# A gated-attention, spectral-mixing and conv-gate kernel: the weight range check moved behind the decode, the low weight parts moved from GpSimd to VectorE

## The chip, the cores and the metric

One core of one Trainium2 chip runs the whole kernel. The metric is the device time of one execution in microseconds (us). Three runs of the kernel before gave 638.92, 641.32 and 641.36 us; the median is 641.32 us. Engines are named as in the profile: PE (TensorE), DVE (VectorE), ACT (ScalarE), POOL (GpSimd), SP (the engine whose queue issues the loads and stores).

## The reference

Three stages follow one another. All inputs are drawn with a fixed seed; the weights are 64-bit floats, the rest 32-bit.

```python
# 1. gated linear attention, per batch (4) and head (8), 768 steps, head size 48
state = alpha[:, :, t, :, None] * state + np.einsum('bhd,bhe->bhde', k[:, :, t], v[:, :, t])
y[:, :, t] = np.einsum('bhd,bhde->bhe', q[:, :, t], state)
# 2. spectral mixing over the 768 tokens, width 384
theta = x @ w_theta
yr = np.einsum('ts,bsd->btd', w_tok_r, x * np.cos(theta))
yi = np.einsum('ts,bsd->btd', w_tok_i, x * np.sin(theta))
u = x + yr + yi
x = u + np.maximum(u @ w_ch, 0.0)
# 3. MLP (384 -> 1024 -> 384) with a 3-tap convolution over tokens as its gate
h = np.maximum(x @ w_in, 0.0)
out = (h * sigmoid(conv(h, conv_w))) @ w_out
```

## The kernel before

Tokens are worked in 24 chunks of 128 (6 for each of 4 batches). The program is written stage by stage, and a scheduler (`schedule_with_timeline_sim=True`, L632) then sets the order of the instructions on each engine. Every engine works its list in order, and each load is issued from SP's list in order too, so that a load that waits for its buffer holds back the loads behind it.

**Attention.** For chunk `ci`, `a_load` brings `a_t`, `qk_t` and `v_t`. `a_prep` works on DVE: a scan backwards (L216), the starts (L219, L220), a scan forwards (L221), a small product (L222), and the product of queries and keys with both scans (L224). ACT then squares the scans in place for a range check (L225); there is one buffer `fbt`, so the next chunk's first scan waits for this. `a_score` and `a_y` are matmuls, with copies on ACT and a triangular mask on POOL (L239); the state is updated on DVE and POOL (L274, L279).

**Mixing.** `a_theta` multiplies a chunk by `w_theta` (tile `th`), takes cosine and sine on ACT and DVE (tile `zf`), and splits the product into a high and a low part (`zh`, `zl`). `m_mix` multiplies these by `w_tok` (tile `yps`). Every fp32 product is made of three matmuls of such parts (`mm3`), so every weight is split too.

**Weights.** A piece of weights is up to 768 64-bit numbers per partition. `load_split` (L110) loads it into one of two buffers (tile `stage`, STB = 2); `decode` (L94) turns it into fp32 in the same buffer, and `split` (L69) writes high and low part. Step by step: POOL squares the upper words as fp32 (L99); ACT takes the sign of the square less a tiny bound and sums it into a column of `wacc` (L103, and an accumulator read of its own); DVE builds the fp32 word in three instructions (L106, L107, L108); ACT copies the high part (L70); POOL subtracts it to give the low part (L71). The DVE steps write where the sign was written, so they wait for it, and the sign waits for the square. The buffer is free for the next load when POOL has subtracted.

There are 24 pieces: 2 of `w_theta` and 12 of `w_tok` while attention runs (batches 0 and 1), 2 of `w_ch`, 4 of `w_in` and, with the MLP under way, 4 of `w_out`. The 3 taps of the convolution (`conv_w`, L404) are decoded without a split. `count_bad` (L502) compares each column of `wacc` with the number of weights in the piece; if one differs, a slow second program runs after the fast one. POOL writes the 25 wanted numbers (L506).

**Channel matmul and MLP.** `m_ch` (tile `cps`) and `m_in`/`m_out` (tiles `hps`, `ops`) follow, with splits on ACT and DVE and the convolution on ACT and DVE (L474 to L488). The low parts of all activations are subtracted on DVE already (the last argument of `split`).

Of the kernel before, what the change touches and what calls it, by code (L numbers as in the profile page):

```python
# [8 lines left out]
F32 = mybir.dt.float32  # L9
# [5 lines left out]
AF = mybir.ActivationFunctionType  # L15
ALU = mybir.AluOpType
PSUM = bass.MemoryType.PSUM

P = 128
# [6 lines left out]
NF = DFF // P  # L26
# [12 lines left out]
TINY = 2.0**-15  # L39
# [3 lines left out]
def tile_gated_linear_attention__then__spectral_moe__then__conv_gate(  # L43
# [14 lines left out]
    nc = tc.nc  # L58
# [10 lines left out]
    def split(hi, lo, src, lo_eng):  # L69
        nc.scalar.copy(hi, src)  # L70
        lo_eng.tensor_tensor(lo, src, hi.bitcast(F32), ALU.subtract)  # L71
# [3 lines left out]
    wacc = top_p.tile([P, 32], F32, name="wacc")  # L75
# [3 lines left out]
    pieces = []  # L79
# [5 lines left out]
    def body(top, slow):  # L85
# [8 lines left out]
        def decode(full, st, n):  # L94
            words = st[:, : 2 * n].bitcast(U32).rearrange("p (n two) -> p n two", two=2)
            lo, hi = words[:, :, 0], words[:, :, 1]
            hif = hi.bitcast(F32)
            fb = full.bitcast(U32)
            nc.gpsimd.tensor_tensor(full, hif, hif, ALU.mult)  # L99
            if not slow:  # L100
                i = len(pieces)
                pieces.append(n)
                nc.scalar.activation(full, full, AF.Sign, bias=ntiny, accum_out=wacc[:, i : i + 1])  # L103
            else:
                nc.vector.scalar_tensor_tensor(hif, full, TINY * TINY, hif, ALU.is_ge, ALU.mult)
            nc.vector.tensor_scalar(fb, hi, 3, 0x3FFFFFFF, ALU.logical_shift_left, ALU.bitwise_and)  # L106
            nc.vector.scalar_tensor_tensor(fb, hi, 0xC0000000, fb, ALU.bitwise_and, ALU.bitwise_or)  # L107
            nc.vector.scalar_tensor_tensor(fb, lo, 29, fb, ALU.logical_shift_right, ALU.bitwise_or)  # L108

        def load_split(pool, tag, src, shape, out_hi, out_lo, scale=None):  # L110
            n = math.prod(shape)
# [11 lines left out]
            split(out_hi, out_lo, full, nc.gpsimd)  # L123
# [5 lines left out]
        with ExitStack() as ph1:  # L129
# [50 lines left out]
            nc.gpsimd.memset(ntiny, -TINY * TINY)  # L180
# [223 lines left out]
            decode(cw.rearrange("p f k -> p (f k)"), cst, 3 * NF)  # L404
            for c in range(NC):
                m_mix(B - 1, 0, c)
# [95 lines left out]
        def count_bad():  # L502
            np_ = len(pieces)
            want = st_p.tile([P, 32], F32, tag="want", name="want", bufs=1)
            for i, n in enumerate(pieces):
                nc.gpsimd.memset(want[:, i : i + 1], float(n))  # L506
            good = st_p.tile([P, 32 + NCH], F32, tag="good", name="good", bufs=1)
            nc.vector.tensor_tensor(good[:, :np_], wacc[:, :np_], want[:, :np_], ALU.is_equal)
# [128 lines left out]
```

## Time and profile before

| | |
|---|---|
| runs | 638.92, 641.32, 641.36 us; median 641.32 us |
| the profiled execution, first to last instruction (span) | 636.5 us; no other time of this execution is given |
| median less span | 4.8 us |
| PE busy | 598.3 us, 94% |
| DVE busy | 472.9 us, 74% |
| ACT busy | 357.2 us, 56% |
| POOL busy | 159.3 us, 25% |

How to read it: a busy engine is one with an instruction under way, so a stretched instruction counts as busy for as long as it stretches. The busy share of PE is modelled and says little of its speed; the number of matmuls in a stretch and the granted clock beside it say more. Shares over the whole span mix stages that have different limits, so each stage is read by itself. The trace has a stretch for each: 0 to 16 us the fill, 16 to 160 attention with weight loads, 160 to 347 attention and mixing without weight loads, 347 to 448 the loads of the other weights with channel matmul and the first MLP units, 448 to the end the MLP.

### The profile page before, as it was taken

To read this page: it belongs to the slowest core of one execution; us is meant where nothing else is said; L and a number is where in the kernel's file an instruction comes from. 1 tells how busy PE (TensorE), PEld (TensorE's weight loads), DVE (VectorE), ACT (ScalarE), POOL (GpSimd) and SP (SyncE) were. 2 spreads that over 40 slices of the span, in tenths; PEclk is the share of its full clock that TensorE was granted. 3 is DMA by queue.
4 is the path that set the end of the run, shared out by engine and by line. 5 is a ranking of instruction groups with operands and counts; after the bars stand their busy time and mean duration, and the time that the engine had idled before them with its cause. 6 is when DMAs were issued, how large, how long until landed. Compare 5 with 4: busy or idle time off the path is not lost.

```text
span 636.5 us, 9621 instructions
## 1 busy us (share of the span) xinstructions
PE 598.3 (94%) x3703; PEld 576.1 (91%) x3703; DVE 472.9 (74%) x699; ACT 357.2 (56%) x713; POOL 159.3 (25%) x166
## 2 busy tenths in 40 slices
PE   6988797889989999999999999799999999999995
PEld 3978796888979999999999999797999999999995
DVE  6889999997885567843147689999987776777760
ACT  3465665454485346743256343754787767766761
POOL 3367556558301131022100343242100000000000
PEclk8577967987999999999999999899999999999998
DMA  8264344543401333021000321230000001000001
GB/s 296 53 204 161 116 158 113 142 158 104 158 1 36 119 125 97 1 75 59 1 0 27 123 77 51 100 94 5 26 25 26 26 13 38 26 13 25 26 26 42
DMA packets 20805, 47.22 MB, mean 74 GB/s; under 512 B 2064, under 2 KB 8208, under 8 KB 20752
## 3 DMA queue, kind: packets, MB, share of 16 engines
q1 hardware_dynamic: 20752, 46.53, 22.6%
q8 instruction: 31, 0.51, 0.4%
q14 instruction: 22, 0.18, 0.1%
HBM read 41.80 MB, written 4.72 MB: 73 GB/s over the span
## 4 chain that ended last, share of the span: by engine, by line
PE 55%; DVE 18%; ACT 4%; issue 3%; DMA 3%; POOL 1%; SPq 0%; ACTq 0%; DVEq 0%; POOLq 0%
PE ops L62 15%; PE hps L62 13%; PE yps L62 12%; PE y L62 5%; PE th L62 3%; DVE stage L107 2%; PE sc L62 2%; DVE qk_t L224 2%; DVE stage L106 2%; DVE stage L108 1%; DVE x L71 1%; PE cps L62 1%; PE kv L62 1%; DVE us L71 1%; DVE fbt L216 1%
## 5 line engine op out<-in xcount | busy, mean ns | idle before, releaser
L62 PE MATMUL yps<-wtok,zh 128*128 128x384 f32 x576 | 155.4, 350 | 2.2 <-DVE u L347 2.2
L62 PE MATMUL hps<-x,win 128*128 128x386 f32 x576 | 111.7, 342 | 4.6 <-ACT hh L474 4.0
L62 PEld LDWEIGHTS yps<-wtok,zh 128*128 128x128 f32 x576 | 108.4, 197 | 2.8 <-ACT zf L316 2.5
L62 PE MATMUL ops<-wout,g 128*128 128x384 f32 x576 | 109.1, 338 | 0.1
L62 PEld LDWEIGHTS hps<-x,win 128*128 128x128 f32 x576 | 103.1, 191 | 6.0 <-ACT hh L474 5.0
L62 PEld LDWEIGHTS ops<-wout,g 128*128 128x128 f32 x576 | 101.8, 187 | 0.6 <-POOL wout L71 0.4
L62 PE MATMUL yps<-wtok,zl 128*128 128x384 f32 x288 | 98.5, 346 | 0.6 <-DVE zl L71 0.6
L239 POOL TENSOR_SCALAR_AFFINE_SELECT pt<-pt 128x512 f32<-128x512 f32 x48 | 39.5, 845 | 141.3 <-ACT pt L238 141.3
L62 PE MATMUL y<-v_t,pt 128*128 128x48 f32 x384 | 60.3, 289 | 1.8 <-issue 1.5
L62 PEld LDWEIGHTS y<-v_t,pt 128*128 128x128 f32 x384 | 57.2, 217 | 2.7 <-issue 1.7
L225 ACT ACTIVATE fbt<-fbt 128x1024 f32<-128x1024 f32 x24 | 25.5, 1062 | 57.3 <-DVE qk_t L224 49.4
L62 PEld LDWEIGHTS yps<-wtok,zl 128*128 128x128 f32 x288 | 56.1, 195 | 0.9 <-DVE zl L71 0.9
L479 DVE SCALAR_TENSOR_TENSOR cv<-hh,cw,cv 128x383 f32<-128x383 f32 (+1 forms) x64 | 43.3, 679 | 17.3 <-ACT cv L476 16.8
L99 POOL TENSOR_TENSOR stage<-stage 128x768 f32<-128x768 f32 (+1 forms) x24 | 41.1, 1717 | 36.4 <-DMA stage<-in_w_out_dram 14.4
L62 PE MATMUL th<-wth,zh 128*128 128x384 f32 x216 | 46.1, 358 | 1.8 <-DVE zh L71 1.8
L71 DVE TENSOR_TENSOR g<-cv,g 128x384 fp32r<-128x384 f32 x64 | 36.4, 569 | 13.3 <-ACT g L70 12.3
L70 ACT CAST g<-cv 128x384 fp32r<-128x384 f32 x64 | 32.7, 510 | 20.7 <-DVE cv L486 19.3
L216 DVE TENSOR_TENSOR_SCAN fbt<-a_t,onehot 128x512 f32<-128x512 f32 x24 | 30.9, 1287 | 16.7 <-ACT fbt L225 13.3
L486 DVE SCALAR_TENSOR_TENSOR cv<-cv,hh 128x384 f32<-128x384 f32 x64 | 36.6, 573 | 8.9 <-ACT cv L485 7.2
L62 PE MATMUL cps<-us,wch 128*128 128x384 f32 x216 | 42.5, 348 | 0.7 <-DVE us L71 0.7
L224 DVE TENSOR_TENSOR qk_t<-qk_t,fbt 128x1024 f32<-128x1024 f32 x24 | 36.4, 1518 | 8.7 <-DMA qk_t<-in_qka_dram 8.4
L476 ACT ACTIVATE cv<-hh,cw 128x384 f32<-128x384 f32 x64 | 39.2, 616 | 6.5 <-DVE g L71 3.8
(91 smaller groups left out, 997.5 us busy)
## 6 DMA issues: line engine op xcount, KB each, us to landing
qk_t<-in_qka_dram SPq DMA_DIRECT2D x24, 512.0 KB, 4.2
stage<-in_w_tok_dram SPq DMA_DIRECT2D x12, 768.0 KB, 4.6
a_t<-in_qka_dram SPq DMA_DIRECT2D x24, 260.0 KB, 2.8
v_t<-in_v_dram SPq DMA_DIRECT2D x24, 192.0 KB, 3.3
out_dram<-ob SPq DMA_DIRECT2D x24, 192.0 KB, 1.9
stage<-in_w_in_dram SPq DMA_DIRECT2D x4, 768.0 KB, 4.9
stage<-in_w_out_dram SPq DMA_DIRECT2D x4, 768.0 KB, 4.4
stage<-in_w_theta_dram SPq DMA_DIRECT2D x1, 768.0 KB, 9.3
```

Source lines behind the costliest of these rows:

```text
L62: nc.tensor.matmul(o, lhsT, rhs, start=start, stop=stop, skip_group_check=True)
L70: nc.scalar.copy(hi, src)
L71: lo_eng.tensor_tensor(lo, src, hi.bitcast(F32), ALU.subtract)
L99: nc.gpsimd.tensor_tensor(full, hif, hif, ALU.mult)
L106: nc.vector.tensor_scalar(fb, hi, 3, 0x3FFFFFFF, ALU.logical_shift_left, ALU.bitwise_and)
L216: nc.vector.tensor_tensor_scan(bf[:, CW - 1 :: -1], ash[:, CW - 1 :: -1], of[:, CW - 1 :: -1], 0.0, ALU.mult, ALU.add)
L224: nc.vector.tensor_tensor(qt, qt, fl, ALU.mult)
L225: nc.scalar.activation(fl, fl, AF.Square, accum_out=bacc[:, ci : ci + 1])
L239: nc.gpsimd.affine_select(pt, pt, [[0, NP], [1, P]], ALU.is_ge, 0.0, base=0, channel_multiplier=-1)
L476: nc.scalar.activation(cv, hh[:, o : o + HALF], AF.Copy, scale=cw[:, f, 1:2])
L479: nc.vector.scalar_tensor_tensor(cv[:, a:HALF], hh[:, o + a - 1 : o + HALF - 1], cw[:, f, 0:1], cv[:, a:HALF], ALU.mult, ALU.add)
L486: nc.vector.scalar_tensor_tensor(cv, cv, 1.0, hh[:, o : o + HALF], ALU.add, ALU.mult)
```

## The change

The square on POOL (L99) is dropped from the fast program, and the sign is no longer ahead of the decode. A new function `judge` stands behind the split: it takes the sign of the upper word less the bound, and the sign of its negative less the bound, in two ACT instructions that read every second word of the buffer, write the other words (the lower ones, used by then), and sum into two columns. Where all weights lie outside the bound, the two sums cancel; `count_bad` adds the columns and compares with zero. The low part of every weight is subtracted on DVE in place of POOL. The buffer is free for the next load when the second sign is done.

```diff
--- before.py
+++ after.py
@@ -72,7 +72,7 @@
 
     top_p = ctx.enter_context(tc.tile_pool(name="top", bufs=1))
     dram_p = ctx.enter_context(tc.tile_pool(name="xd", bufs=1, space=bass.MemoryType.DRAM))
-    wacc = top_p.tile([P, 32], F32, name="wacc")
+    wacc = top_p.tile([P, 2, 32], F32, name="wacc")
     bacc = top_p.tile([P, NCH], F32, name="bacc")
     flag = top_p.tile([1, 1], I32, name="flag")
     x_dram = dram_p.tile([B, S, DM], F32, name="x_dram")
@@ -96,16 +96,23 @@
             lo, hi = words[:, :, 0], words[:, :, 1]
             hif = hi.bitcast(F32)
             fb = full.bitcast(U32)
-            nc.gpsimd.tensor_tensor(full, hif, hif, ALU.mult)
-            if not slow:
-                i = len(pieces)
-                pieces.append(n)
-                nc.scalar.activation(full, full, AF.Sign, bias=ntiny, accum_out=wacc[:, i : i + 1])
-            else:
+            if slow:
+                nc.gpsimd.tensor_tensor(full, hif, hif, ALU.mult)
                 nc.vector.scalar_tensor_tensor(hif, full, TINY * TINY, hif, ALU.is_ge, ALU.mult)
             nc.vector.tensor_scalar(fb, hi, 3, 0x3FFFFFFF, ALU.logical_shift_left, ALU.bitwise_and)
             nc.vector.scalar_tensor_tensor(fb, hi, 0xC0000000, fb, ALU.bitwise_and, ALU.bitwise_or)
             nc.vector.scalar_tensor_tensor(fb, lo, 29, fb, ALU.logical_shift_right, ALU.bitwise_or)
+
+        def judge(st, n):
+            if slow:
+                return
+            words = st[:, : 2 * n].rearrange("p (n two) -> p n two", two=2)
+            i = len(pieces)
+            pieces.append(n)
+            for j, sgn in enumerate((1.0, -1.0)):
+                nc.scalar.activation(
+                    words[:, :, 0], words[:, :, 1], AF.Sign, bias=ntiny, scale=sgn, accum_out=wacc[:, j, i : i + 1]
+                )
 
         def load_split(pool, tag, src, shape, out_hi, out_lo, scale=None):
             n = math.prod(shape)
@@ -120,7 +127,8 @@
                 nc.scalar.activation(full, full, AF.Copy, scale=scale)
             if len(shape) == 2:
                 full = full.rearrange("p (a n) -> p a n", a=shape[0])
-            split(out_hi, out_lo, full, nc.gpsimd)
+            split(out_hi, out_lo, full, nc.vector)
+            judge(st, n)
 
         ub, xs, zs = {}, {}, {}
 
@@ -177,7 +185,7 @@
             nc.vector.memset(onehot, 0.0)
             nc.vector.memset(onehot[:, :, P - 1 : P], 1.0)
             nc.vector.memset(starts, 0.0)
-            nc.gpsimd.memset(ntiny, -TINY * TINY)
+            nc.gpsimd.memset(ntiny, -TINY)
             for t in Sst:
                 nc.gpsimd.memset(t, 0.0)
             nc.gpsimd.memset(magic, MAGIC)
@@ -402,6 +410,7 @@
             cst = st_p.tile([P, 9 * 256], F32, tag="w", name="cst", bufs=STB)
             nc.sync.dma_start(out=cst[:, : 6 * NF].bitcast(U32), in_=conv_w.rearrange("p f k -> p (f k)").bitcast(U32))
             decode(cw.rearrange("p f k -> p (f k)"), cst, 3 * NF)
+            judge(cst, 3 * NF)
             for c in range(NC):
                 m_mix(B - 1, 0, c)
             tok0_ctx.close()
@@ -501,11 +510,10 @@
 
         def count_bad():
             np_ = len(pieces)
-            want = st_p.tile([P, 32], F32, tag="want", name="want", bufs=1)
-            for i, n in enumerate(pieces):
-                nc.gpsimd.memset(want[:, i : i + 1], float(n))
+            both = st_p.tile([P, 32], F32, tag="both", name="both", bufs=1)
+            nc.vector.tensor_tensor(both[:, :np_], wacc[:, 0, :np_], wacc[:, 1, :np_], ALU.add)
             good = st_p.tile([P, 32 + NCH], F32, tag="good", name="good", bufs=1)
-            nc.vector.tensor_tensor(good[:, :np_], wacc[:, :np_], want[:, :np_], ALU.is_equal)
+            nc.vector.tensor_scalar(good[:, :np_], both[:, :np_], 0.0, None, ALU.is_equal)
             nc.vector.tensor_scalar(good[:, np_ : np_ + NCH], bacc, BIG, None, ALU.is_le)
             bad = st_p.tile([P, 2], F32, tag="bad", name="bad", bufs=1)
             nc.vector.tensor_reduce(bad[:, 0:1], good[:, : np_ + NCH], mybir.AxisListType.X, ALU.min)
```

The scheduler orders the new list anew. Three places show what moves. `stage` is a weight buffer, `fbt` the scans, `qk_t` queries and keys, `wtok` the split token weights; a number behind a name tells buffers and chunks apart.

DVE, near the last pieces of `w_tok`. Before, the last piece is decoded just ahead of the product of the 14th chunk (`qk_t_1264`):

```order
L106 TENSOR_SCALAR stage_1320<-stage_1320 128x768
L107 SCALAR_TENSOR_TENSOR stage_1320<-stage_1320 128x768
L274 TENSOR_TENSOR tst_1223<-S0_112,kv_1218 112x384
L108 SCALAR_TENSOR_TENSOR stage_1320<-stage_1320 128x768
L71 TENSOR_TENSOR zh_1432<-u_857,zh_1432 128x384
L224 TENSOR_TENSOR qk_t_1264<-qk_t_1264,fbt_1608 128x1024
```

Now it is decoded and split ahead of the product of the 11th chunk (`qk_t_986`):

```order
L102 TENSOR_SCALAR stage_1320<-stage_1320 128x768
L71 TENSOR_TENSOR wtok11_88<-stage_1232,wtok10_87 128x2x384
L103 SCALAR_TENSOR_TENSOR stage_1320<-stage_1320 128x768
L224 SCALAR_TENSOR_TENSOR fbt_1084<-a_t_984,onehot_110 128x512
L104 SCALAR_TENSOR_TENSOR stage_1320<-stage_1320 128x768
L282 TENSOR_TENSOR tst_948<-S1_113,kv_943 112x384
L71 TENSOR_TENSOR zl_777<-zf_770,zh_757 128x768
L227 TENSOR_SCALAR starts_111<-fbt_1084 128x4
L228 RECIPROCAL starts_111<-starts_111 128x4
L229 SCALAR_TENSOR_TENSOR fbt_1084<-a_t_984,starts_111 128x512
L230 TENSOR_TENSOR ftot_1085<-a_t_984,fbt_1084 128x4
L71 TENSOR_TENSOR wtok11_88<-stage_1320,wtok10_87 128x2x384
```

All weight work of the attention stage stands some three chunks earlier, and the chunks behind it follow one another on DVE with no weight work between them.

ACT, at the fourth and fifth piece of `w_tok`, as it is now:

```order
L70 CAST wtok00_85<-stage_543 128x2x384
L113 ACTIVATE stage_543,wacc_60<-stage_543,ntiny_75 128x768
L233 ACTIVATE fbt_581,bacc_61<-fbt_581 128x1024
L324 ACTIVATE zf_466<-th_456,magic_114 128x384
L113 ACTIVATE stage_543,wacc_60<-stage_543,ntiny_75 128x768
L70 CAST wtok00_85<-stage_635 128x2x384
L113 ACTIVATE stage_635,wacc_60<-stage_635,ntiny_75 128x768
```

The two signs of a piece stand behind its high part, one ahead of the square of the scans (L233) and one behind it.

SP, the loads around the same pieces. Before, a load of `stage` waits for POOL:

```order
L116 DMA stage_444<-in_w_tok_dram 128x2x768 [waits DMAHW7_49,Pool_49]
L116 DMA stage_543<-in_w_tok_dram 128x2x768 [waits DMAHW0_49,Pool_49]
L199 DMA qk_t_577<-in_qka_dram 128x1024 [waits DMAHW1_49,PE_49]
L201 DMA v_t_480<-in_v_dram 128x384 [waits DMAHW2_49,PE_49]
L197 DMA a_t_801<-in_qka_dram 128x520 [waits DMAHW3_49,DVE_49]
```

Now it waits for ACT:

```order
L123 DMA stage_543<-in_w_tok_dram 128x2x768 [waits DMAHW7_49,Activation_49]
L207 DMA qk_t_478<-in_qka_dram 128x1024 [waits PE_49]
L209 DMA v_t_381<-in_v_dram 128x384 [waits PE_49]
L123 DMA stage_635<-in_w_tok_dram 128x2x768 [waits DMAHW0_49,DMAHW3_49,DVE_49,Activation_49]
L205 DMA a_t_667<-in_qka_dram 128x520 [waits DMAHW1_49,DVE_49]
```

The loads of the same pieces stand one to two chunks earlier among the loads of `qk_t`, and what holds them is the second sign.

## Rows read from the trace of the kernel before

**Rows 1.** Busy us by stretch: PE, PEld, DVE, ACT, POOL (instructions), PEclk, DMA share, GB/s.
```profile
16.00:160.00 144.00, 126.55 (x780) 118.53 (x779) 132.96 (x153) 79.37 (x155) 87.00 (x61) 0.78 0.43 134
160.00:192.00 32.00, 29.81 (x200) 28.30 (x199) 25.60 (x37) 20.97 (x40) 6.30 (x5) 1.00 0.23 74
192.00:347.00 155.00, 155.00 (x1132) 150.85 (x1131) 81.96 (x124) 77.10 (x149) 22.99 (x38) 1.00 0.18 53
...
384.00:448.00 64.00, 58.59 (x305) 55.16 (x304) 61.52 (x94) 34.59 (x72) 22.23 (x12) 0.95 0.16 53
448.00:608.00 160.00, 160.00 (x911) 159.72 (x910) 124.68 (x229) 114.50 (x241) 0.48 (x1) 1.00 0.07 25
```
**Rows 2.** The chain that ended last: start us, us, what.
```profile
123.18 2.86 DVE qk_t L224
```
**Rows 3.** DVE groups, 16 to 176 us: count, busy us, mean ns, idle before.
```profile
L224 DVE TENSOR_TENSOR qk_t<-qk_t,fbt 128x1024 f32<-128x1024 f32 x14 | 24.1, 1725 | 1.8 <-DMA qk_t<-in_qka_dram 1.6
...
L107 DVE SCALAR_TENSOR_TENSOR stage<-stage 128x768 uint32<-128x768 uint32 (+1 forms) x14 | 15.7, 1129 | 0.1
L106 DVE TENSOR_SCALAR stage<-stage 128x768 uint32<-128x768 uint32 (+1 forms) x14 | 14.0, 1002 | 2.5 <-ACT stage L103 2.4
...
L321 DVE TENSOR_TENSOR zf<-x,zf 128x768 f32<-128x768 f32 x6 | 10.8, 1796 | 0.5 <-ACT zf L320 0.5
...
L219 DVE TENSOR_SCALAR starts<-fbt 128x4 f32<-128x4 f32 x14 | 7.0, 501 | 0.3
L222 DVE TENSOR_TENSOR ftot<-a_t,fbt 128x4 f32<-128x4 f32 x13 | 6.5, 502 | 1.7 <-POOL S L279 1.7
```
**Rows 4.** DVE groups, 192 to 347 us, where no weights are worked on.
```profile
L321 DVE TENSOR_TENSOR zf<-x,zf 128x768 f32<-128x768 f32 x14 | 13.4, 958 | 7.0 <-ACT zf L320 6.9
L71 DVE TENSOR_TENSOR zl<-zf,zh 128x768 fp32r<-128x768 f32 x13 | 12.3, 954 | 2.0 <-ACT zh L70 2.0
L224 DVE TENSOR_TENSOR qk_t<-qk_t,fbt 128x1024 f32<-128x1024 f32 x8 | 9.8, 1229 | 6.8 <-DMA qk_t<-in_qka_dram 6.8
...
L222 DVE TENSOR_TENSOR ftot<-a_t,fbt 128x4 f32<-128x4 f32 x9 | 1.5, 165 | 6.1 <-POOL S L279 6.0
...
L219 DVE TENSOR_SCALAR starts<-fbt 128x4 f32<-128x4 f32 x8 | 1.4, 171 | 0.2
```
**Rows 5.** All weight pieces' decode steps: ns min/median/max, first and last start us.
```profile
L106 DVE TENSOR_SCALAR stage<-stage x24: 351/552/2106, 18.4 to 438.9; 128x768 uint32<-128x768 uint32 x22, 128x384 uint32<-128x384 uint32 x2
L107 DVE SCALAR_TENSOR_TENSOR stage<-stage x24: 550/957/2504, 22.5 to 441.0; 128x768 uint32<-128x768 uint32 x22, 128x384 uint32<-128x384 uint32 x2
```
**Rows 6.** POOL in order of time at 379 us, then DVE at the same time.
```profile
378.75 1.85 POOL L71 TENSOR_TENSOR win<-stage,win 128x768 fp32r<-128x768 f32 x1 [4.04 <-ACT win L70]
380.56 1.78 POOL L99 TENSOR_TENSOR stage<-stage 128x768 f32<-128x768 f32 x1
...
379.12 4.11 DVE L71 TENSOR_TENSOR x<-u,x 128x386 fp32r<-128x386 f32 x3 [0.39 <-ACT x L70]
...
383.62 0.55 DVE L71 TENSOR_TENSOR x<-u,x 128x386 fp32r<-128x386 f32 x1
```
**Rows 7.** POOL groups, 16 to 176 us.
```profile
L71 POOL TENSOR_TENSOR wtok<-stage,wtok 128x768 fp32r<-128x768 f32 x12 | 27.2, 2267 | 22.6 <-ACT wtok L70 22.2
L99 POOL TENSOR_TENSOR stage<-stage 128x768 f32<-128x768 f32 x12 | 23.9, 1995 | 8.8 <-DMA stage<-in_w_tok_dram 8.6
L239 POOL TENSOR_SCALAR_AFFINE_SELECT pt<-pt 128x512 f32<-128x512 f32 x24 | 22.8, 969 | 14.8 <-ACT pt L238 14.8
L279 POOL TENSOR_TENSOR S<-tst,ftot 48x192 f32<-48x192 f32 x16 | 16.0, 999 | 6.7 <-DVE tst L274 3.3 <-ACT kt L247 2.6
```
**Rows 8.** ACT groups, 16 to 176 us.
```profile
L103 ACT ACTIVATE stage<-stage,ntiny 128x768 f32<-128x768 f32 (+1 forms) x13 | 11.8, 910 | 5.4 <-POOL stage L99 5.4
L70 ACT CAST wtok<-stage 128x768 fp32r<-128x768 f32 x12 | 10.0, 834 | 13.7 <-DVE stage L108 13.7
...
L103 ACT ACTIVATION_READ_ACCUMULATOR stage<-stage,ntiny 128x1 f32 x14 | 2.7, 190 | 0.0
```

## The prediction, made before the changed kernel ran

> **What bounds the kernel now.** I read the stretches first, then the chain, then the engines' groups, and last two engines side by side in time. The stretches [rows 1] show two limits. From 192 to 347 us and from 448 to 608 us PE is busy throughout at the full granted clock (1.00, the upper of its two levels, 2.4 GHz) while DVE is busy 82 of 155 and 125 of 160 us: nothing that DVE, ACT or POOL do there sets the time. From 16 to 160 us it is the other way: DVE is busy 133 of 144 us, PE's granted clock is 0.78 and it finishes 780 matmuls in 144 us (5.4 per us) against 1132 in 155 (7.3 per us) of about the same mixture behind. This is the front stage, in which attention and 14 of the 24 weight pieces share DVE. From 160 us on PE is nearly full again (29.8 of 32 us, clock 1.00). The second stretch with a loss is 384 to 448 us: 305 matmuls in 64 us, which at the MLP's rate (911 in 160 us, 5.69 per us) would take 53.6 us, so some 10 us are lost there, and DVE is busy 61.5 of the 64 us. The chain of waits agrees: between 101 and 182 us it is mostly DVE, and one of its steps is a product of 2.86 us [rows 2] that elsewhere takes 1.23 [rows 4]. So the time is set by DVE in two stages and by PE in the rest; a microsecond taken from DVE in the first comes back until PE is the limit, and in the second up to 10 us.
>
> **Why DVE is so full.** The same instructions take longer in the front stage than where no weights are worked on. Counts times the undisturbed mean, taken from the busy time [rows 3, 4, 5]: L224 24.1 - 14 x 1.229 = 6.9 us; L106 14.0 - 14 x 0.552 (its median) = 6.3; L321 10.8 - 6 x 0.958 = 5.1; L219 7.0 - 14 x 0.171 = 4.6; L222 6.5 - 13 x 0.165 = 4.4; L107 15.7 - 14 x 0.957 = 2.3. Together 29.6 us, in which DVE counts as busy and does nothing more. What they run beside is seen at 379 us: three subtractions of 0.55 us each (1.65) take 4.11 us, while POOL goes through a subtraction and a square of 1.85 and 1.78 us; they end as POOL ends [rows 6]. Instructions of four elements (L219, L222) are drawn out to half a microsecond on average, so it is waiting and not slower work.
>
> **The change, part by part, front stage (14 pieces).**
> - POOL loses its square and its subtraction. Which part of the 29.6 us goes with them is not shown by a row, so it is bounded: none (the remaining mask and state updates stretch DVE as much), or all. Between: what an instruction waits behind another grows with that one's length, so I weigh POOL's busy time with its mean length [rows 7]: L71 27.2 x 2.27 = 62 and L99 23.9 x 2.00 = 48, against L239 22.8 x 0.97 = 22 and L279 16.0 x 1.00 = 16. The two that go have 110 of 148, 74%. I take 22 us.
> - DVE gains the 14 subtractions. The same form is there, 128x768 from two fp32 operands in 0.954 us [rows 4]: 12 of `w_tok` and one of `w_theta` at that, one half as long, 12.9 us. All of it counts, since DVE is the limit there.
> - DVE no longer waits for the sign ahead of L106: 2.4 us in this stage [rows 3].
> - ACT: the sign moves behind the decode and becomes two, each with its accumulator read: 14 x (0.910 + 0.190) = 15 us more [rows 8]. ACT's 79 of 144 us [rows 1] become some 95. This is covered while ACT is the looser engine; not covered, it is rival 2. New in it is that the sign reads every second word. No ACT row shows that; a gain is excluded, as it handles the same 768 elements; the bounds are 0.91 us as now and 1.82 us, as if it walked over the skipped words too. I take 0.91, because DVE's L107 reads every second word and its median is 0.957 us, no more than the 0.954 us of the subtraction on packed words [rows 4, 5].
> - The wait that is added: a load of `stage` now waits for the second sign, and behind it in SP's list wait loads of `a_t` and `qk_t`, which DVE needs. From the end of the decode that is a high part and two signs, 0.83 + 2 x 1.10 = 3.0 us on ACT [rows 8], against high part and POOL's subtraction, 0.83 + 2.27 = 3.1 us, before [rows 7, 8]; and the square and sign ahead of the decode (2.0 + 1.1 us) are gone. So a buffer turns round about 3 us sooner, if ACT takes the signs at once. I cost it at nothing; its cover is that 3 us.
> - The order: the weight pieces now end ahead of the 11th chunk's product instead of the 14th's. It shifts work within the stage and adds none. The preparations behind run alone, and each then waits for ACT's square of the one `fbt`; I allow 1 us for that.
>
> Sum for the front stage: -22 + 12.9 - 2.4 + 1 = about -10.5 us. PE can follow: at its rate behind (7.3 per us) the 780 matmuls would take 107 of the 144 us, and from 160 us on it is bound by itself, so what DVE gains ahead is gained.
>
> **Weight stage (347 to 448 us, 10 pieces).** POOL does nothing there but this. The three splits at 379 us alone lose 4.11 - 1.65 = 2.5 us to it [rows 6]. Against that stand 10 subtractions on DVE, 9.1 us, and 11 us more of ACT, which is busy 35 of 64 us [rows 1]. Each piece has two steps fewer on POOL between its landing and its use. The gain is at most PE's 10 us of loss, and it is below nothing if the 9.1 us weigh more on DVE than what goes; I take half of the loss, 5 us, since DVE is relieved and loaded at once and the earlier weights let PE start the MLP sooner.
>
> **Without effect.** 25 fills of `want` on POOL and the comparison at the end of `count_bad`: nothing waits for them until the flag is read. The MLP from 448 us and the stretch 192 to 347 us: PE's, untouched.
>
> Total: 10.5 + 5 = about 16 us off. The profiled execution's span of 636.5 us becomes about 620.5; the median of the runs stands 4.8 us above that span, which I leave: **625 us**.
>
> **The rivals.**
> 1. *More comes back.* All 29.6 us go, and groups I left out add some; PE loses nothing in the weight stage. -29.6 + 12.9 - 2.4 = -19, and -10: 612 us. For it: POOL's remaining instructions are themselves drawn out. Against: they stay, and so does what they cost DVE.
> 2. *ACT takes DVE's place.* All the weight work of the front stage now falls into its first two thirds, and ACT with it. Each high part, sign and square stands in one list; a sign of up to 1.82 us adds up to 28 x 0.91 = 25 us to ACT there. Then DVE waits for high parts and squares, and the load queue for the second sign: the front stage gains 2 us instead of 10.5, the weight stage keeps its 5: 634 us. For it: the order puts a sign ahead of the square. Against: ACT has some 50 us to spare.
> 3. *Slower: DVE is full and is given more.* The delays stay and move to the POOL instructions that remain, so DVE has 12.9 us more in the front stage and PE as much longer to wait, less the 2.4; the weight stage loses some 4: 641 + 10.5 + 4 = 656 us. It decides where less than 10.5 of the 29.6 us go. Against it: the mask and the state update are half as long as what goes [rows 7], and in 192 to 347 us they are there and L224 and L219 keep 1.229 and 0.171 us [rows 4]. The Trainium skill (Perfetto Trace Analysis, Optimizing Scalar/DVE Operations) speaks for this rival: where VectorE is saturated, move work off it to ScalarE or even GpSimd; the change does the opposite, and by that rule the stage would lengthen. The same passage adds that moving work between those two might not help because they share a read port; the 4.11 us of three subtractions [rows 6] fit that half.
> 4. *It does not do what it says.* If the two sums did not cancel for weights in range, the slow program would run behind the fast one and the time would be a multiple. For a weight beyond the bound the signs are +1 and -1, whatever the sign of the weight.
>
> **How the numbers follow.** The forecast 0.50; rival 1 0.18; rival 2 0.15; rival 3 0.08; rival 4 0.01; and 0.08 that gains and waits about cancel. About 0.5% (3.2 us) is what a measurement here can tell from no change. Faster: 0.50 + 0.18 + 0.15 = 0.83; same 0.08; slower 0.09. The range of 610 to 640 holds the forecast with its bounds, rivals 1 and 2 and half of the undecided case; outside stay rival 3, rival 4 and some of each end, together under 0.2.
>
> **What would show it.** Right: L224, L219, L222 and L321 near 1.23, 0.17, 0.17 and 0.96 us in the front stage; the weights' subtraction on DVE near 0.95 us; POOL without L99 and L71; PE full from about 150 us instead of 160; more matmuls per us where 384 to 448 us was. Wrong: those means stay up (rival 3); the sign well over 0.94 us, or DVE idle behind ACT's squares and high parts, or behind `qk_t` loads (rival 2); matmuls slower in the MLP, where I expect no change.

## The result, and the profile after

The changed kernel takes 615.48 us (median of 4 runs, 613.1 to 618.19) against 640.12 us (median of 4, 638.14 to 641.36): a ratio of 0.962, with a 95% interval of 0.9589 to 0.9651. The forecast was 625 us in a range of 610 to 640. The profiled execution has a span of 612.1 us, 3.4 us under the median; before it was 636.5. That is 24.4 us less.

Where they went is read from three points of the trace. The first load of `w_ch`, with which the weight stage begins, moves from 347.4 to 333.3 us: the front stage gives 14.1 us. From there to the start of the last matmul of `ops` it was 281.9 us (629.3 less 347.4) and is 272.2 (605.5 less 333.3): the weight stage gives 9.7. The remaining 0.6 us lie in the tail. Before, then after:

```profile
L116 SPq DMA_DIRECT2D stage<-in_w_ch_dram x2: 379/424/468, 347.4 to 347.8; - x2
L62 PE MATMUL ops<-wout,g x576: 331/338/443, 418.8 to 629.3; 128*128 128x384 f32 x192
```
```profile
L123 SPq DMA_DIRECT2D stage<-in_w_ch_dram x2: 379/420/462, 333.3 to 333.7; - x2
L62 PE MATMUL ops<-wout,g x576: 331/338/343, 401.4 to 605.5; 128*128 128x384 f32 x192
```

The stretches, with the columns of [rows 1]:

```profile
16.00:160.00 144.00, 124.32 (x865) 116.64 (x865) 124.53 (x179) 100.85 (x197) 42.72 (x40) 0.87 0.49 151
160.00:192.00 32.00, 32.00 (x224) 30.93 (x224) 21.37 (x32) 22.30 (x42) 3.10 (x6) 1.00 0.09 24
...
384.00:448.00 64.00, 63.34 (x358) 62.17 (x357) 58.23 (x112) 47.69 (x101) 0.00 (x0) 1.00 0.11 35
```

In the front stage PE finishes 865 matmuls instead of 780, its granted clock is 0.87 instead of 0.78, and DVE issues 179 instructions instead of 153 in less busy time (124.5 against 133.0 us). From 384 to 448 us there are 358 matmuls instead of 305, which is 5.59 per us, near the 5.69 of the MLP [rows 1]; counted from the stage's own start, 14 us earlier (370 to 434 us), there are 358 too. POOL is idle there.

When PE becomes the limit is seen in finer windows of the changed kernel:

```profile
112.00:124.00 12.00, 10.27 (x74) 8.87 (x74) 11.10 (x16) 9.47 (x18) 4.46 (x4) 0.86 0.47 145
124.00:136.00 12.00, 11.64 (x97) 11.00 (x97) 9.07 (x16) 6.15 (x13) 3.69 (x5) 1.00 0.34 102
136.00:148.00 12.00, 12.00 (x93) 11.64 (x92) 6.29 (x12) 4.80 (x10) 4.29 (x8) 1.00 0.47 158
```

PE is full from about 125 us, where DVE falls from 11.1 to 9.1 and then 6.3 of 12 us. The DVE groups of 16 to 160 us, which hold the same 14 chunks as [rows 3]:

```profile
L232 DVE TENSOR_TENSOR qk_t<-qk_t,fbt 128x1024 f32<-128x1024 f32 x14 | 17.5, 1252 | 2.7 <-DMA qk_t<-in_qka_dram 2.6
L224 DVE TENSOR_TENSOR_SCAN fbt<-a_t,onehot 128x512 f32<-128x512 f32 x14 | 17.5, 1252 | 5.7 <-ACT fbt L233 5.7
L103 DVE SCALAR_TENSOR_TENSOR stage<-stage 128x768 uint32<-128x768 uint32 (+1 forms) x13 | 13.3, 1027 | 0.0
...
L71 DVE TENSOR_TENSOR wtok<-stage,wtok 128x768 fp32r<-128x768 f32 x12 | 11.7, 972 | 0.0
L102 DVE TENSOR_SCALAR stage<-stage 128x768 uint32<-128x768 uint32 x12 | 7.2, 601 | 3.2 <-DMA stage<-in_w_tok_dram 3.2
...
L329 DVE TENSOR_TENSOR zf<-x,zf 128x768 f32<-128x768 f32 x6 | 5.9, 975 | 0.0
...
L227 DVE TENSOR_SCALAR starts<-fbt 128x4 f32<-128x4 f32 x14 | 3.6, 254 | 0.1
...
L230 DVE TENSOR_TENSOR ftot<-a_t,fbt 128x4 f32<-128x4 f32 x13 | 2.4, 187 | 2.9 <-POOL S L287 2.9
...
L71 DVE TENSOR_TENSOR wth<-stage,wth 128x768 fp32r<-128x768 f32 (+1 forms) x2 | 1.5, 752 | 0.0
```

The product of queries and keys takes 1.252 us on average instead of 1.725, the product with `zf` 0.975 instead of 1.796, the four-element instructions 0.254 and 0.187 instead of 0.501 and 0.502. The subtraction that came to DVE takes 0.972 us. POOL and ACT in the same stretch, answering to [rows 7] and [rows 8]:

```profile
L247 POOL TENSOR_SCALAR_AFFINE_SELECT pt<-pt 128x512 f32<-128x512 f32 x24 | 27.4, 1159 | 94.2 <-ACT pt L246 94.1
L287 POOL TENSOR_TENSOR S<-tst,ftot 48x192 f32<-48x192 f32 x16 | 15.4, 962 | 7.2 <-DVE tst L282 6.5
```
```profile
L113 ACT ACTIVATE stage<-stage,ntiny 128x768 f32<-128x768 f32 (+1 forms) x28 | 27.6, 988 | 0.0
...
L113 ACT ACTIVATION_READ_ACCUMULATOR stage<-stage,ntiny 128x1 f32 x28 | 5.5, 195 | 0.0
```

The chain of waits (start, length, what) still runs over DVE up to 112 us, but its product step of 2.86 us [rows 2] is now one of 1.23, and ACT has come into it with signs:

```profile
110.18 1.23 DVE qk_t L232
111.41 0.88 DVE stage L104
112.31 0.83 ACT wtok L70
113.14 0.98 ACT stage L113 x2
...
115.16 0.72 ACT zh L70
115.88 1.00 ACT stage L113 x2
```

### The profile page after: what moved, and what is told of

It is laid out like the page before. It is cut to its first block, busy times and chain, and to the rows that moved or that the text cites. A ratio compares the mean times of both kernels' runs of the same rounds, so it can differ in the third digit from the quotient of the medians.

```text
span 612.1 us, 9575 instructions
## 1 busy us (share of the span) xinstructions
PE 578.9 (95%) x3703; PEld 561.1 (92%) x3703; DVE 442.2 (72%) x724; ACT 381.5 (62%) x763; POOL 69.3 (11%) x92
## 4 chain that ended last, share of the span: by engine, by line
PE 60%; DVE 10%; issue 7%; DMA 5%; ACT 3%; ACTq 0%; POOLq 0%; DVEq 0%; SPq 0%
PE ops L62 16%; PE hps L62 14%; PE yps L62 13%; PE y L62 6%; PE th L62 3%; PE sc L62 3%; DMA stage<-in_w_in_dram 2%; PE cps L62 2%; PE kv L62 2%; ACT stage L113 2%; DMA stage<-in_w_out_dram 1%; DVE stage L104 1%; DVE stage L103 1%; PE kps L253 1%; DVE us L71 1%
## 5 line engine op out<-in xcount | busy, mean ns | idle before, releaser
L62 PE MATMUL yps<-wtok,zh 128*128 128x384 f32 x576 | 150.7, 344 | 10.6 <-ACT zh L70 10.3
L62 PEld LDWEIGHTS yps<-wtok,zh 128*128 128x128 f32 x576 | 105.3, 192 | 12.1 <-ACT zh L70 11.3
L247 POOL TENSOR_SCALAR_AFFINE_SELECT pt<-pt 128x512 f32<-128x512 f32 x48 | 44.6, 948 | 218.7 <-ACT pt L246 218.6
L62 PE MATMUL y<-v_t,pt 128*128 128x48 f32 x384 | 56.5, 276 | 0.0
L233 ACT ACTIVATE fbt<-fbt 128x1024 f32<-128x1024 f32 x24 | 25.4, 1059 | 46.8 <-DVE qk_t L232 45.6
L62 PEld LDWEIGHTS y<-v_t,pt 128*128 128x128 f32 x384 | 53.3, 204 | 0.8 <-POOL pt L247 0.3
L488 DVE SCALAR_TENSOR_TENSOR cv<-hh,cw,cv 128x383 f32<-128x383 f32 (+1 forms) x64 | 39.3, 618 | 18.0 <-ACT cv L485 17.5
L113 ACT ACTIVATE stage<-stage,ntiny 128x768 f32<-128x768 f32 (+1 forms) x48 | 47.0, 979 | 0.2
L494 ACT ACTIVATE cv<-cv 128x384 f32<-128x384 f32 x64 | 33.3, 520 | 17.3 <-DVE cv L491 17.1
L246 ACT COPY pt<-sc 128x512 f32<-128x512 f32 x48 | 25.8, 584 | 27.5 <-PE y L62 27.4
L224 DVE TENSOR_TENSOR_SCAN fbt<-a_t,onehot 128x512 f32<-128x512 f32 x24 | 29.8, 1241 | 17.4 <-ACT fbt L233 15.5
L483 ACT ACTIVATE hh<-hps 128x386 f32<-128x386 f32 x64 | 31.5, 492 | 16.1 <-PE hps L62 16.0
```

The lines of the kernel that those rows point to most:

```text
L62: nc.tensor.matmul(o, lhsT, rhs, start=start, stop=stop, skip_group_check=True)
L113: nc.scalar.activation(words[:, :, 0], words[:, :, 1], AF.Sign, bias=ntiny, scale=sgn, accum_out=wacc[:, j, i : i + 1])
L224: nc.vector.tensor_tensor_scan(bf[:, CW - 1 :: -1], ash[:, CW - 1 :: -1], of[:, CW - 1 :: -1], 0.0, ALU.mult, ALU.add)
L233: nc.scalar.activation(fl, fl, AF.Square, accum_out=bacc[:, ci : ci + 1])
L246: nc.scalar.copy(pt, scs[j])
L247: nc.gpsimd.affine_select(pt, pt, [[0, NP], [1, P]], ALU.is_ge, 0.0, base=0, channel_multiplier=-1)
```

## The experiments

**Theory A:** DVE's lost time is the stretch that POOL's long two-operand instructions put on whatever DVE has under way; the subtraction taken to DVE costs its own 13 us there and frees more. **Rival B:** the gain is of another kind: the pieces end earlier, or POOL's queue no longer holds back masks and loads. Each comparison is with the kernel before on the same chip; medians of before were 641.15 (first four), 641.13 (next four) and 640.14 us (last three).

To put a number on the stretch, each DVE instruction between 16 and 180 us is compared with the median of its form where POOL ran nothing beside it, and the excess is booked to the POOL instruction that lies longest beside it. This is worked out from the traces of the profiled executions, as are the starts of the weight stage; the times are medians. The profiled executions of e10 and e7 took 634.7 and 633.7 us, over their medians.

| kernel | time, us | stretch on DVE | of it by POOL's subtraction / square / added work | weight stage starts |
|---|---|---|---|---|
| before | 640.1 | 35.5 | 17.8 / 10.6 / - | 347.4 |
| e1, check moved alone | 634.5 | 23.0 | 19.1 / - / - | 348.3 |
| e2, subtraction moved alone | 622.3 | 20.2 | - / 11.3 / - | 338.6 |
| after, both | 615.5 | 6.0 | - | 333.3 |
| e3, two-operand work added | 656.0 | 35.8 | - / - / 30.2 | 362.0 |
| e10, copies added | 629.7 | 18.1 | - / - / 13.1 | 350.0 |
| e4, no check | 610.2 | 6.8 | - | 330.8 |
| e7, four signs | 631.3 | 4.2 | - | 347.0 |

**Each part alone (e1, e2).** e1 is the changed kernel with POOL subtracting again; e2 is the kernel before with DVE subtracting.

```diff
 e1
-            split(out_hi, out_lo, full, nc.vector)
+            split(out_hi, out_lo, full, nc.gpsimd)
 e2, from the kernel before
-            split(out_hi, out_lo, full, nc.gpsimd)
+            split(out_hi, out_lo, full, nc.vector)
```

> The changed kernel with the weights' low parts subtracted on POOL again; the check stays behind the decode. Theory A (what POOL does beside DVE stretches DVE): the square is gone and its share of the stretch with it, the subtraction's share stays and DVE is spared the 12.9 us of subtractions: about 622 to 630 us, with the products L232 and the L329 products still above 1.3 us in the front stage. Theory B (the gain came from the shorter way of a piece from landing to use, and POOL's work beside DVE costs little): the square and sign are off that way and the subtraction is as it was before: 612 to 618 us, as the changed kernel or better, since DVE has less to do.

Measured: 634.53 us (632.17 to 636.46), ratio 0.9913 [0.9879, 0.9947]. Above what either theory gave.

> The kernel before with the weights' low parts subtracted on DVE; the square on POOL and the one sign stay ahead of the decode. Theory A: the subtraction's share of the stretch (42% by length, some 12 us in the front stage) goes and 12.9 us of subtractions come, the square's share stays: 632 to 640 us. Theory B: the way of a piece is a little shorter (0.95 for 2.27 us), so 628 to 636 us. Both parts alone add up to less than the whole if the order of the weights matters, since with the sign ahead of the decode the pieces stay late in DVE's list.

Measured: 622.27 us (619.87 to 624.12), ratio 0.9716 [0.9675, 0.9758]. Below what either gave. DVE groups of e1 from 16 to 160 us, and POOL's beside them:

```profile
L102 DVE TENSOR_SCALAR stage<-stage 128x768 uint32<-128x768 uint32 x12 | 15.0, 1251 | 2.7 <-DMA stage<-in_w_tok_dram 2.3 <-POOL S L287 0.4
...
L329 DVE TENSOR_TENSOR zf<-x,zf 128x768 f32<-128x768 f32 x6 | 7.4, 1227 | 0.6 <-ACT zf L328 0.6
L227 DVE TENSOR_SCALAR starts<-fbt 128x4 f32<-128x4 f32 x12 | 6.0, 500 | 0.2
```
```profile
L71 POOL TENSOR_TENSOR wtok<-stage,wtok 128x768 fp32r<-128x768 f32 x12 | 26.1, 2173 | 28.7 <-ACT wtok L70 28.5
```

With the square gone the first decode step still takes 1.251 us and the four-element one 0.500. The subtraction is the costlier of the two: on POOL it puts 19.1 us of stretch on DVE, on DVE it takes 13.2 us of its own (11.7 + 1.5). I had expected e1 to be better than e2, or about equal; the order is the reverse. The two parts also differ by stage. The front stage (start of the weight stage) moves by +0.9 us with the check alone, by -8.8 with the subtraction alone and by -14.1 with both; so the check's move pays there only where POOL's subtraction is gone. From the start of the weight stage to the end it is 289.1 us before, 283.5 in e1, 281.8 in e2 and 278.8 with both: the two gains, 5.6 and 7.3, add to 12.9 and give 10.3, where PE's whole loss had been read as some 10. In e2 the pieces stand late among the chunks, as before, so the earlier order that came with the moved check is not what the gain needs. Nor is that order enough: e1 has it too (its last piece of `w_tok` is decoded at 122.7 us, against 160.4 before and 117.4 after). Two stretches of e1, with the columns of [rows 1]:

```profile
16.00:160.00 144.00, 118.97 (x759) 111.05 (x759) 121.32 (x150) 94.24 (x184) 60.98 (x49) 0.79 0.44 133
136.00:148.00 12.00, 12.00 (x108) 11.35 (x106) 7.00 (x13) 5.51 (x11) 2.19 (x4) 1.00 0.34 106
```

DVE has 12.5 us less stretch than before and is busy 11.6 us less (121.3 against 133.0), yet PE finishes no more matmuls (759 against 780) and the stage is no shorter. From 136 us PE is full, so what DVE is spared there shortens nothing; why PE was given less work before that is open. A microsecond of stretch taken away is thus not always a microsecond of the stage.

**The subtraction by stage (e5, e6).** The same argument of `split` is chosen by the pool's tag, "st" for the attention stage.

```diff
 e5
-            split(out_hi, out_lo, full, nc.vector)
+            split(out_hi, out_lo, full, nc.vector if tag == "st" else nc.gpsimd)
 e6
-            split(out_hi, out_lo, full, nc.vector)
+            split(out_hi, out_lo, full, nc.gpsimd if tag == "st" else nc.vector)
```

> The changed kernel, with the low parts of the 14 attention-stage pieces subtracted on VectorE and those of the pieces behind on GpSimd again. Theory A (the gain is two separate terms, about 14 us in the front stage and about 5 of the 10 us of the weight stage, both from the stretch that GpSimd's subtraction puts on VectorE): the front stage as in the changed kernel, the weight stage starting near 333 us; the weight stage 5 us longer, as it was with all subtractions on GpSimd; 619 to 622 us. Rival B (the subtraction matters little in the front stage): 626 us or more, the weight stage starting near 345 us or later.

Measured: 619.87 us (618.4 to 621.46), ratio 0.969 [0.9648, 0.9733]; the weight stage starts at 332.9 us. As A.

> The reverse: the 14 attention-stage pieces subtracted on GpSimd, the later ones on VectorE. Theory A: no gain in the front stage (weight stage starting near 348 us), the weight stage as in the changed kernel; 628 to 631 us. Rival B: 619 to 624 us.

Measured: 630.59 us (629.66 to 631.05), ratio 0.9849 [0.9807, 0.989]; the weight stage starts at 348.3 us. As A. Against the changed kernel the subtraction is worth 15.1 us in the front stage and 4.4 in the weight stage. Their sum, 19.5, is close to e1's distance of 19.05. e5, whose front stage is the changed kernel's, also shows that the granted clock is not what sets its length: 0.82 here against 0.87, with as many matmuls (867 and 865) and the weight stage starting within 0.4 us.

```profile
16.00:160.00 144.00, 130.42 (x867) 122.91 (x867) 125.66 (x179) 100.94 (x197) 39.85 (x40) 0.82 0.49 151
```

**The suspected cost put back (e3, e10).** POOL works twice per piece on the finished high part, into a tile that nobody reads: two-operand products and differences in e3, copies (one operand) in e10.

```diff
 e3
+        scr = const.tile([P, 768], BF16, name="scr")
...
             split(out_hi, out_lo, full, nc.vector)
             judge(st, n)
+            if not slow:
+                hi, dst = out_hi.bitcast(F32), scr[:, :n]
...
+                nc.gpsimd.tensor_tensor(dst, hi, hi, ALU.mult)
+                nc.gpsimd.tensor_tensor(dst, hi, hi, ALU.subtract)
 e10, from e3
-                nc.gpsimd.tensor_tensor(dst, hi, hi, ALU.mult)
-                nc.gpsimd.tensor_tensor(dst, hi, hi, ALU.subtract)
+                nc.gpsimd.tensor_copy(dst, hi)
+                nc.gpsimd.tensor_copy(dst, hi)
```

> The changed kernel, and beside it POOL does two more instructions per piece of the same size (768 numbers, two fp32 operands: a product and a difference of the high part, written to a scratch tile that nobody reads). No buffer and no engine waits for them except POOL's own mask and state updates. Theory A: DVE is stretched again, by 20 to 30 us in the front stage, and 10 us in the weight stage: 630 to 642 us. Theory B: nothing waits for these, 615 to 619 us.

Measured: 655.96 us (654.35 to 656.96), ratio 1.0237 [1.0202, 1.0272]. A's direction and more of it: 40 us over the changed kernel, for work whose result nobody reads. (A's own terms, 20 to 30 us and 10 us over the changed kernel, add up to 645 to 656 us; its range of 630 to 642 was added up wrongly.) Here are DVE's and POOL's groups of e3:

```profile
L71 DVE TENSOR_TENSOR wtok<-stage,wtok 128x768 fp32r<-128x768 f32 x12 | 17.4, 1446 | 0.0
...
L237 DVE TENSOR_TENSOR ftot<-a_t,fbt 128x4 f32<-128x4 f32 x10 | 5.4, 540 | 1.2 <-POOL S L294 1.2
```
```profile
L138 POOL TENSOR_TENSOR scr<-wtok 128x768 bf16<-128x768 f32 x12 | 24.2, 2019 | 0.7
L137 POOL TENSOR_TENSOR scr<-wtok 128x768 bf16<-128x768 f32 x12 | 23.8, 1986 | 25.0 <-ACT wtok L70 24.9
```

The four-element product is back at 0.540 us and DVE's new subtraction goes from 0.972 to 1.446. The stretch grows by 29.8 us, and the front stage by 28.7 (362.0 less 333.3). Nothing waits for these POOL results. Masks and state updates stand behind them in POOL's list, but from 16 to 176 us the trace shows no wait of PE for a mask and 1.4 us for the state (1.6 in the changed kernel), so B's reason has no part in it.

> As the kernel with two products and differences per piece on GpSimd into a tile nobody reads, but each of them replaced by a copy of the high part (one operand read instead of two). Theory A (what stretches VectorE is GpSimd reading two operands): 616 to 622 us, VectorE's stretch in the front stage under 12 us. Rival B (any long GpSimd instruction does it): 640 us or more, stretch near 30 us.

Measured: 629.71 us (627.51 to 634.68), ratio 0.9835 [0.9796, 0.9874]. Between the two. POOL's groups of e10:

```profile
L137 POOL CAST scr<-wtok 128x768 bf16<-128x768 f32 x12 | 18.1, 1506 | 6.4 <-ACT wtok L70 6.1
...
L138 POOL CAST scr<-wtok 128x768 bf16<-128x768 f32 x12 | 14.8, 1230 | 0.5
```

All copies are 37.3 us of POOL in this stretch and put 13.1 us of stretch on DVE (35%); e3's two-operand work is 54.9 us and puts 30.2 (55%). So one operand costs DVE less per microsecond of POOL, but not nothing, and my sharp line between one and two operands does not hold.

**The check's price on ACT (e4, e7).** e4 sets `wacc` to zero once and takes no sign, so the range of the weights is not checked; e7 takes each pair twice.

```diff
 e4
         def judge(st, n):
-            if slow:
+            if not slow and not pieces:
+                nc.vector.memset(wacc, 0.0)
+                pieces.extend([n] * 25)
+            if True:
                 return
 e7
-            for j, sgn in enumerate((1.0, -1.0)):
+            for j, sgn in enumerate((1.0, -1.0, 1.0, -1.0)):
...
-                    words[:, :, 0], words[:, :, 1], AF.Sign, bias=ntiny, scale=sgn, accum_out=wacc[:, j, i : i + 1]
+                    words[:, :, 0], words[:, :, 1], AF.Sign, bias=ntiny, scale=sgn, accum_out=wacc[:, j % 2, i : i + 1]
```

> The changed kernel without the two signs: the weights' range is not checked (the sums are set to zero once). If ACT's 33 us of signs in the front stage are covered: 612 to 616 us, the front stage shorter by less than 3 us. If ACT is what holds the front stage now (rival 2 in part): 603 to 610 us, with DVE's waits for squares, high parts and loads of weights smaller.

Measured: 610.22 us (608.43 to 614.84), ratio 0.9544 [0.949, 0.9599]. Between the two forecasts, and its runs overlap with those of the changed kernel (613.1 to 618.19): by the medians the signs cost 5.3 us, by the spans of the profiled executions 3.4 (612.1 less 608.7), of which 2.5 lie in the front stage (333.3 less 330.8).

> The changed kernel with each pair of signs taken twice (four sums per piece, of which the last two count). Theory A (ScalarE has cover, and a pair of signs costs what leaving it out gave back, about 5 us): 618 to 622 us. Rival B (ScalarE, busy 101 of 144 us in the front stage, has no cover for 28 to 33 us more, so that squares, high parts and loads come late): 626 to 640 us.

Measured: 631.31 us (630.0 to 633.7), ratio 0.9854 [0.981, 0.9898]. As B. By the medians the first pair costs 5.3 us, the second 15.8. In e7, from 16 to 160 us, ACT has become the busier engine, and DVE waits for loads whose buffer the signs hold:

```profile
16.00:160.00 144.00, 123.03 (x791) 115.64 (x790) 114.96 (x166) 120.96 (x242) 35.12 (x38) 0.79 0.44 137
```
```profile
L102 DVE TENSOR_SCALAR stage<-stage 128x768 uint32<-128x768 uint32 x12 | 6.9, 576 | 9.6 <-DMA stage<-in_w_tok_dram 9.6
```

The changed kernel stands at ACT 100.9 us of 144 with 3.2 us of such waits; 20 us of ACT more, and the front stage is 13.7 us longer (347.0 less 333.3). SP's queue waits 34.1 us for signs there, against 5.6 in the changed kernel.

**Three tries at a better version (e8, e9, e11).** e8 gives the scans a third half, so that a chunk's backward scan need not wait for the square; e9 copies the high parts of the attention stage on POOL instead of ACT; e11 does the state update on DVE.

```diff
 e8
+            scans = None if slow else sc_p.tile([P, 3, CW], F32, name="scans")
...
-                fbt = sc_p.tile([P, 2, CW], F32, tag="fbt", name="fbt")
-                fo, bf = fbt[:, 0], fbt[:, 1]
+                alt = 1 + ci % 2
+                fo, bf = scans[:, 0], scans[:, alt]
...
-                fl = fbt.rearrange("p b t -> p (b t)")
+                fl = scans[:, 0 : alt + 1 : alt]
...
 e9
-            split(out_hi, out_lo, full, nc.vector)
+            if tag == "st" and not slow:
+                nc.gpsimd.tensor_copy(out_hi, full)
+                nc.vector.tensor_tensor(out_lo, full, out_hi.bitcast(F32), ALU.subtract)
...
 e11
-                        (nc.gpsimd if c > 0 else nc.vector).tensor_tensor(
+                        nc.vector.tensor_tensor(
```

> The changed kernel with a third half in the scan buffer, so that a chunk's backward scan does not wait for ScalarE's square of the chunk before. Theory A (in the front stage VectorE is still the limit until about 125 us, and its 5.7 us of waiting for the square come back at least by half): 610 to 613 us. Rival B (VectorE's waits there are not the limit any more, or the wait moves to the next release): 614 to 617 us.

Measured: 621.96 us (619.98 to 622.91). Slower than the changed kernel, outside both. The wait for the square went from the backward to the forward scan (5.7 to 3.8 us), and others grew:

```profile
L234 DVE TENSOR_TENSOR qk_t<-qk_t,scans 128x1024 f32<-128x1024 f32 x12 | 16.0, 1329 | 4.8 <-DMA qk_t<-in_qka_dram 4.7
L230 DVE TENSOR_TENSOR_SCAN scans<-a_t,starts 128x512 f32<-128x512 f32 x13 | 15.8, 1218 | 3.9 <-ACT scans L235 3.8
...
L231 DVE TENSOR_TENSOR ftot<-a_t,scans 128x4 f32<-128x4 f32 x13 | 2.1, 160 | 5.8 <-POOL S L289 5.7
```

> The changed kernel, with the high parts of the 14 attention-stage pieces copied on GpSimd in place of ScalarE. Theory A (ScalarE is close to its limit there, since two signs more cost 16 us and two signs less give 5; an instruction of GpSimd that reads one operand stretches VectorE little): ScalarE loses 14 x 0.83 us, 610 to 614 us. Rival B (GpSimd takes the copies late, in order behind its masks, and VectorE's subtraction waits): 617 to 625 us.

Measured: 621.04 us (618.3 to 623.46). B's time, but not by B's reason: DVE's subtraction waits only 0.7 us for POOL's copy, while DVE's stretch goes from 6.0 to 14.8 us; the copies lie beside 5.6 of it. So it was also wrong that a one-operand instruction of POOL stretches DVE little.

> The changed kernel with the state update (two-operand product of 48x192) on VectorE throughout. Theory A (VectorE is given 16 x 0.354 = 5.7 us in the front stage and gets back 2.9 of waiting for the state and some 2 of stretch): 614 to 617 us. Rival B (the state comes sooner for TensorE too and the chunks' chain shortens): 608 to 613 us.

Measured: 619.1 us (617.44 to 619.94). Outside both: DVE waits 6.5 us for `kv` ahead of `tst`, where it was 0.6, and 4.5 us for loads of `qk_t`, where it was 2.6.

Each of the three edits made the scheduler order the list anew, so how much of their loss is the edit and how much the order is open. No version that keeps the check beat the changed kernel; e11's runs overlap with its runs.

## Why the prediction was right, point by point

- **DVE stretched by POOL, the mechanism.** Right. e3 brings it back by itself, e5 and e6 place it in both stages. The direction rests on this. The prediction read that the three subtractions at 379 us end as POOL ends; the first two do, and the third is not stretched (0.55 us).
- **"I take 22 us" of the 29.6 us.** Under-sized. By the same arithmetic on the six groups after, with the same undisturbed means, about 3.4 us are left (1.2 in L227, 0.9 in L103, 0.6 in L102, the rest 0.3 or less each), so 26 went. The weighing by POOL's busy time and length gave mask and state update 26% of the stretch; by the table they had 7.1 of 35.5 us before (20%) and 6.0 after, so the weighing was near. Over all groups of DVE 29.5 us went (35.5 less 6.0): the six groups did not hold all of the stretch.
- **14 subtractions, 12.9 us.** 13.2 measured.
- **The wait of 2.4 us for the sign.** Gone, but in its place the first decode step waits 3.2 us for loads of `stage`, and the backward scan 5.7 us for the square, where it was 4.1 on the trace of before. Some of this falls behind 125 us, where PE is the limit and it costs nothing.
- **The sum of the front stage, -10.5.** Measured -14.1. That the total came near is in part luck, because the sum does not hold for the parts. Stretch that went, subtractions that came and the wait of 2.4 us for the sign (gone in all three) give -12.5 - 2.4 = -14.9 us for e1, -15.3 + 13.2 - 2.4 = -4.5 for e2 and -29.5 + 13.2 - 2.4 = -18.7 for both; measured are +0.9, -8.8 and -14.1. The step that a microsecond taken from DVE in the front stage comes back until PE is the limit holds in e3 (29.8 us of stretch, 28.7 of stage) and not in e1. PE was full from about 125 us and not from 150, but e1, with the same early order, is full from 136 us and gains nothing, so this is not shown to be the reason for the excess. It stays open what e1 lost and e2 gained beyond the sum.
- **ACT, costed at nothing.** Too low. A sign takes 0.988 us and not 0.91 (28 signs: 2.2 us more), ACT is at 100.9 us against my 95, and e4 puts the price of the signs at 3.4 to 5.3 us. What rival 2 describes is real: e7 shows that another 20 us of ACT cost 15.8 us, by the wait for the load queue that it named.
- **The load that waits for the second sign, costed at nothing.** Its cover holds in the changed kernel (DVE waits 3.2 us for these loads), and is used up in e7 (9.6 us).
- **The weight stage, "half of the loss", -5.** Measured -9.7, nearly all of PE's loss (at 5.69 per us the 358 matmuls take 62.9 of the 64 us). The reason I gave for halving it, that DVE is relieved and loaded at once, did not hold: DVE had room for the 10 subtractions once the stretch was gone (58.2 of 64 us busy, with 112 instructions instead of 94).
- **MLP and 192 to 347 us unchanged.** Right. Counted 14 us earlier, the changed kernel runs 1137 matmuls from 178 to 333 us and 912 from 434 to 594, against 1132 and 911 before [rows 1]; e5 and e6 run 912 and 911 from 448 to 608 us.
- **Rival 1 (612 us)** came nearest in time. The result lies between it and the forecast: its front stage of -19 was too much, its weight stage of -10 was right.
- **Rival 3 (slower).** It decides where less than 10.5 of the 29.6 us go; 26 went. DVE was full and was given more, and the stage got shorter. The rule I weighed there (the Trainium skill, Perfetto Trace Analysis, Optimizing Scalar/DVE Operations: where VectorE is saturated, offloading to ScalarE or even GpSimd may make sense) did not hold here: e2 does only the opposite and gains 18.9 us. Its caution that moving work between these two might not help is borne out: on POOL the subtraction puts 17.8 us of stretch on DVE, on DVE it takes 13.2.
- **Rival 4 (not doing what it says).** Did not occur: nothing of the slow program stands in the trace, whose span is 612.1 us.

## What to carry to other kernels

Before an elementwise step is given to GpSimd to relieve VectorE, compare two numbers of the trace: what the step takes on VectorE alone, and by how much VectorE's other instructions are longer than their undisturbed selves while GpSimd has it. Very short instructions that take half a microsecond on average are the sign to look for; a full VectorE may be a waiting one. Then measure each part of a change by itself: e1 took 12.5 us of stretch away and the stage became no shorter. And when a step is moved to an engine with room, check how much room is left: the first pair of signs cost a third of what the second did.

## What the runs showed of the hardware

The stretch depends on the POOL instruction. Two-operand ones of 128x768 put 55% of their own time on DVE as stretch (30.2 of 54.9 us in e3), one-operand copies of the same size 35% (13.1 of 37.3 in e10), masks 17% (4.6 of 27.4 in the changed kernel). The number of operands does not order them alone: the square of the kernel before, which reads its one tensor twice, put 44% (10.6 of 23.9 [rows 7]), and the state updates, with two operands of 48x192, 12% (1.9 of 15.4 in the changed kernel). All shares follow from the booking above and are estimates. DVE instructions with one SBUF operand are stretched as well, L102 from 0.601 to 1.251 us and the four-element L227 from 0.254 to 0.500 in e1.

The Trainium skill (SBUF — State Buffer, SBUF: two separate sides) describes the port pair that the two engines share as an exclusive lock, where the other one fully blocks for the whole instruction. That four-element instructions are drawn out to 0.5 us fits it. So does DVE at 379 us in the kernel before, where the first two subtractions of [rows 6] stand in finer windows as

```profile
379.12 1.90 DVE L71 TENSOR_TENSOR x<-u,x 128x386 fp32r<-128x386 f32 x1 [0.39 <-ACT x L70]
380.94 1.82 DVE L71 TENSOR_TENSOR x<-u,x 128x386 fp32r<-128x386 f32 x1
```

They end at 381.02 and 382.76 us, each 0.42 us behind an instruction of POOL (380.60 and 382.34), and the third, beside no POOL work, takes 0.55. That equally sized copies cost DVE a smaller share than two-operand work is not told by that sentence. By the same section a DVE instruction meets the lock with two SBUF operands or in a two-port mode; L102 and L227 read one tensor operand. L102 is L106 of the kernel before, whose median is 0.552 us against 0.957 of L107 for as many elements [rows 5], which would fit such a mode; no run here shows in which mode they ran.

A sign that reads every second word takes 0.988 us, a sign on packed words 0.910 [rows 8]. And POOL's masks did not become shorter when POOL was emptied: their mean in the front stage went from 0.969 [rows 7] to 1.159 us, while DVE beside them was faster.
